# Attention and a gated feed-forward block in one launch: moving the DMA transposes to TensorE, and the copies of the sinks' values to SyncE's queue

## The chip, the core and the metric

The kernel runs on one core of one Trainium2 chip. The metric is the device time in microseconds, from a handful of runs of the compiled kernel. Beside them there is one execution that was taken by the hardware profiler; its span, its rows and its waits are what the views below show.

## The reference

Two parts, one after the other, float32 in and out.

```
scores = (q @ k^T) / 8                       # 4 batches, 8 heads, 768 positions, head dim 64
heads 0, 2, 6 : causal mask                  # the "retrieval" heads
other heads   : causal and (key < 4  or  query - key < 64)   # 4 sinks and a window of 64
x = softmax(scores) @ v   ->  3072 rows x 512
out = (silu(x @ w_gate) * (x @ w_val)) @ w_out       # 512 -> 1536 -> 512
```

## The kernel before

**Tiles.** The rows are cut into 24 tiles of 128 queries. Two neighbouring tiles of a batch make a pair; there are 12 pairs, of which pairs 0 to 5 belong to batches 0 and 1 and pairs 6 to 11 to batches 2 and 3. Four tiles make a group, and the feed-forward part runs by group: six groups of 512 rows.

**Attention of a pair.** SyncE loads 512 KB each of q, k and v (`load`, L341) into one of 11 buffers `raw`. An engine casts q and k to float16 into `hq` (`cast`, L429), and v into `vt` (`castv`, L446). q and k must then be turned, so that the head dimension lies on the partitions (`qT`, `kT`). This is done in two ways:

- pairs 0 to 4 (`XPE = 5`, L336): eight TensorE transposes of 128x128 into one PSUM bank (`transposes`, L469), and two copies out of it by ScalarE or VectorE (`evac`, L475);
- pairs 5 to 11: two transposing DMAs on SyncE's queue (`dmat`, L462), for q as for k. They leave the queries in another order, and `exps` (L569) puts that right by the way it reads and writes (L576).

TensorE then makes the scores (`scores`, L551, its matmuls at L567), ScalarE the exponentials (L579), VectorE or GpSimd multiplies by a mask (L587), TensorE multiplies by the values (`values`, L591, L597), and VectorE divides by the sum into `xb` (`norm`, L600).

**Sinks.** A streaming head sees four sink keys at the start of its batch, and a window. Once a middle tile of a batch has been used, four of its key rows are spent. The keys and values of the sinks are copied into them, so that later tiles find sinks and window in one block of 128 keys. `sinks_v` (L502) does it for the values: two copies of 2 partitions x 330 float16, by VectorE, GpSimd or ScalarE, as the plan says. There are 16 such tiles, hence 32 copies. The `values` of the next tile of the batch wait for them.

**The turned x.** `xb` must be turned too (`xtranspose`, L609). For tiles 0 to 7 (`XBAR = 8`, L423) four TensorE transposes and one copy out of PSUM do it (`xevac`, L624); for tiles 8 to 23 one transposing DMA on SyncE's queue.

**Feed-forward of a group.** For each of 12 slices of 128 columns TensorE makes gate and value products (`gate`, L755, matmuls at L759), ScalarE the tanh (L765), and VectorE two combining steps (L769, L775). The output product is done for groups 0 to 4 with seven half-size products in place of eight (`seventh`, L830, L839; sums of operands at L826, sums of results at L855), for the last group plainly (`outproj`, L788, L793).

**The order.** Everything is a task in a list (`P.add`). The strings `ORDER`, `WAYS` and `SLOTS` were worked out beforehand: `ORDER` gives the tasks in sequence as numbers of two digits to the base 62, `WAYS` the engine of each, `SLOTS` its buffer. Each engine, and SyncE's queue of DMAs, works through its own tasks strictly in that sequence. A number from 3700 up is no task but some filler matmuls on TensorE (`warm`, L315). So a task that waits holds up all that stands behind it on its engine.

Of the kernel before, what the change touches and what calls it, by code (L numbers as in the profile page):

```python
# [13 lines left out]


ORDER = (
    "0306071W091U1V1X000A08xy1c0D0C01050B1d1e040gy01f1gzJ1i1h2021282922232B1j1r1s021p1q1w0F2C2D2E2F1b"
    "2A2L2M2N2O2X2f2g0m1Y1a1Z1t1u1v1k0h252h1l1m2W2c242G2H2I2d2e2l2m2i2j0G271n1o1y1z3C262P2Q2R0z2t3031"
    "2J0y8e8o2n2K102U2o2p3I3J2V8t8j8m8u8v8k8l8n1x2k8f8g8p8q2x382y8h8i118r8s8w8x138y8z9893909495999A33"
    "340n9D9E0E2Z3K3D3L3M3N149B9C9F969G9H972a9192322b2Y2q2r2s2u3R3S3W3X0k1C9c9d9e9h9i9j3U3V3O2z353P36"  # L20
    "39370q1D9f9g9k9l3T3b3i3n3o3f3g0H3H3E3F2v2w0i169I9J9K9N9O9P0o179L9Q9R9M0l1F3Q3Y3Z3c3j3a0I3u40410j"
    "193k3h9m9n9o3l3m3A3B9S9T9U9r9s9t3d3e9X0J3v4344453G3p3q3r0r1G9u9p9v429Y9Z3s3t0x1H2S4647494A4H0p1A"
    "9V9WB74N4O4Q4R0K3z9q9zA10N4c3x4BB4B5B6B8Ak4K4L4V4b4C4D3yAT484M0w0sAQARASAU9a9b9y0t1E0W6K2TAlAmAV"
    "AWAX151M1O1N1PAYAZBEAfAgAhB9BABB4a0u181Q1R1SBCBDAp0v1BBFBGA0AaAbAnAoAc3wBHBIAdAe0L0M0PB20T12A41I"
    "1J1K0S4d4P0O4Z4h4g4Y4e4f5D5L5K0RAzB0B1AqArB31L0YALAM0ZAN4E4F4G4J4I6J1TAuAvAOAPAw9wA2A69xA3A7A55C"
    "5I5JAA4l4m4i4j4kACA8A9ABAD4n4v51524y53AiAj5f5lAEBMAGAFAK4S4z504T4W4UAxAy5g5nAsAtBL4q4r4o4p54BO0c"
    "AHAIAJ4s554t4u4x4wBJBKBQ56575T5U6MBNBP5W5c5XBb5j0X58595A5B707S7T6xBVBW6wBRBS5i5VBXBYBc6z5YBZBaBd"
    "5p5qBT5s605t5u4XBsBtBuCeCbCcCdCfCMCNCOCCBvBwCDCE0V6I5v0Q5F5G5H6v5k5o5M5N5O0UBiBjBk5rCPCQBlBm5E5Z"
    "5a5b5d5wCHCICJCWCXCY5m63696A666768Bh5h73CKCLC7C8C9710eCRCS5P5Q5R6465CACBCTBUC2C36y7Q6P74BnBo5x5y"
    "5z610a72CZCaBp5S625e6H6NBqBrC46B6C6F6D6GCFCGCiBeBfBgBxByBz7O7UC0C1C5C681CUCVCjCl6E6U6V6W6X6Y6R6S"  # L30
    "6T6eDmDjDkDlDnDoDpDqDrDs0b7P7X7WDtDuDv6Z6aCgChCn6b6c6d6fDUDVDWDXDY7576776g7C7D7E7F7G7L0dDwDxCkCm"
    "DSDFDGDHDPDQDRDT7b7c7d6QDADBDCDyDzE0DDDE7H80D5D6D7CsCt6O6n6o6h6i6j6kE1E27V7I7J7M7K7ND8D96l6m7879"
    "7A7BCoCpCrCuCv897Y7Z6p6q8786DKDLDMDZDaDb6L6r6s6t6uDcDdDeDfDgCwCx7e7f7R7j7m7n7o7p7q7rDNDOCyCzD0D4"
    "EhEiEjErEsEcEd88EkElEtCqD1D2D3EuEvEeDhDi7a7g7h7k7iFLFMFNFOFP7x8D8E8A8I8B8C8F8JFJFGFHFIFKFBFCFDDI"
    "DJE5E77s7t8GFEFFEp7u7v7y7w8HEXEYEZ0f838485EmEnEoEqEfEg8NEw8Y8ZE6E88T8U8VEzExEyF0EBE3E9E4EAECEDF6"
    "828K8L8M8OF1F2F3F9EFEG8Q8R8S8W8XEVEHEIEJF7F8FA7l8P7z8a8b8cEaEbESETEUEWEEEOELEM8dGiGMGTGUEKGCENER"
    "G7GVGWGjGkGJGKEPGREQFTFVGXGLGOGPGEGFGNGQG9F4GAGSGGGYGbGZF5GaGcGBGDFSGHFpFqFrFQFRG4G5GdGeFzFUFeFW"
    "FXGIG6G0G8FcFdGfFfFuFvFYFaFbGgGhG1G2G3FsFtFxGlGmFZFwFyFlFiFjFmFnFgFhFkFoGnGoGpGsGtGuGvGwGqGrGxGy"
    "GzH0H2H3H4H5H7H1H6H8H9"
)  # L40
WAYS = (
    "000010000000000000000000000000000000000000000000000000000000221202202202212200200111000111110010"
    "222200001100000000000000220022122022001011000000000000001100212002000011001001000001000001001000"
    "000201021120001000001001000000010010000010000000002221220000000000010000002000100100000020000221"
    "000000000100000002000010010000000000020200000010000000000000110000011000000100100000020001000000"
    "002202200220000000000000000012000100100000000201120000000000000000010002202202010000001001000001"
    "200000000000011002021000000000000000000200000000000000000000000000000000000000000000000000000000"
    "000000000000000000000000000000000000000000001000000000000000000000000000000000000000000000000000"
    "000000000000000000000000000000001000000010000000000000000000000000000000000000000000000000000000"
    "000000000000000000001110100011000000000001000000000000000000000000000000000000000000000000000000"  # L50
    "000000001111000001100000000000100000000000000000000000000000000000000000000000000000000000000111"
    "101100110000000000011000000000000000000000000000000000000000000000000000000000000000010000100000"
    "00000010"
)
SLOTS = (
    "0014237653916A152371476981504A39A2564807049A28352A9168410016041002241601230163620442561014104122"
    "636011642065221025144416322211256461406003404624344620616540610143626540604164236062324342142254"
    "041614064616325426212246140636104325614261306242452460436460636014122636230644521206164434062601"
    "020211341120003102001134000210400214105510131201001011040122021303213020111113411111040020200051"
    "014110101310002114301212131010022102320210013012111032112010000012000102211130011112010111054125"  # L60
    "001050101010110200030111402521014010311140310020120011321112001301101022015010340000101100015042"
    "1331142120102320202014112511225023512531113120100101201"
)
DIGITS = "0123456789ABCDEFGHIJKLMNOPQRSTUVWXYZabcdefghijklmnopqrstuvwxyz"

# [54 lines left out]
def kernel(  # L120
# [13 lines left out]
    nc = tc.nc  # L134
# [198 lines left out]

    XPE = 5  # L336
    XOLD = 1

    landed = {}
# [80 lines left out]
                                 (lambda i=i, x=x: wsum(i, x)),  # L420
                                 deps=[T_w["o", i][0], T_w["o", i + 3][0]] + before))

    XBAR = 8  # L423

    LEAD = 4

    hqs = {}
# [29 lines left out]
    def turned(n, kd):  # L457

        b, pi = QP[n]
        return qT[n % QB] if kd == "q" else kT[b % 2][:, 2 * pi:2 * pi + 2]  # L460

    def dmat(n, kd, m):  # L462
        nc.sync.dma_start_transpose(
            out=turned(n, kd)[:, m].rearrange("c k r (j n) -> c (k r j) n", j=2),
            in_=hqs[n, kd][m * 64:(m + 1) * 64].rearrange("p k a x -> p (k a x)"))

    trs = {}

# [33 lines left out]
    def sinks_v(b, m):  # L502
        V = vt[b % 2]
        for j in range(2):
            rows = slice(j * 64, j * 64 + NSINK // 2)
            recast(T_sv[b, m], V[rows, m, STREAMS], V[rows, 0, STREAMS])

    def plan(t):

# [59 lines left out]
    def exps(t, u, unit):  # L569
        e = es[t, u] = buf("e", [128, 8, 128], FH, "e")  # L570
        for p, s_, c, kt in unit[0]:
            h = PAIRS[p][s_]
            av_blocks.setdefault((t, h), []).append((e[:, c, :], value(t, h, kt)))
        at = slice(min(c for _, _, c, _ in unit[0]), unit[1])
        to, src = e[:, at], whole_sc.pop((t, u))[:, at]
        if t // 2 >= XPE:  # L576
            to = to.rearrange("p c (n j) -> p c n j", j=2)
            src = src.rearrange("p c (j n) -> p c n j", j=2)
        nc.scalar.activation(out=to, in_=src, func=AF.Exp, scale=scale)  # L579

    def mask(task, t, u, m):
# [27 lines left out]
    def xtranspose(t):  # L609
        xb = xbs.pop(t)  # L610
        g, n = GROUP[t]
        if g not in xts:
            xts[g] = buf("xt", [128, 4, 512], FH, "xt")
        if t >= XBAR:
            nc.sync.dma_start_transpose(
                out=xts[g][:, :, n * 128:(n + 1) * 128],
                in_=xb.rearrange("p a b d -> p (a b d)"))
            return
        tr = buf("gv", [128, 4, 128], FH, "xtr")
        for p in range(4):  # L620
            nc.tensor.transpose(tr[:, p, :], xb[:, p].rearrange("p a d -> p (a d)"), ident)
        trs[t] = tr
# [11 lines left out]
    def tasks_of_pair(n):  # L634
# [20 lines left out]
                P.uses(T_iss["x", n], "raw", c)  # L655
        for kd in "qk":
            old = oldq if kd == "q" else older
            if n >= XPE:
                T_ev[n, kd] = [P.lands(P.add(
                    f"d{kd}{n}.{m}", ["SP"], (lambda n=n, kd=kd, m=m: dmat(n, kd, m)),  # L660
                    deps=cs[kd] + old)) for m in range(2)]
                P.uses(cs[kd][0], "hq", *T_ev[n, kd])
                continue
            tr = P.add(f"tr{kd}{n}", ["PE"], (lambda n=n, kd=kd: transposes(n, kd)),
                       deps=cs[kd], takes=["gv"], after=[T_warm])
            T_ev[n, kd] = []
# [8 lines left out]
    def tasks_of_tile(t):  # L675
# [50 lines left out]
        if 1 <= i < NT - 1:  # L726
            T_sk[b, i] = P.add(f"sk{b}.{i}", ["DVE", "POOL", "ACT"],
                               (lambda b=b, i=i: sinks_k(b, i)), deps=own)
            T_sv[b, i] = P.add(f"sv{b}.{i}", ["DVE", "POOL", "ACT"],
                               (lambda b=b, i=i: sinks_v(b, i)), deps=T_v_of[b, i])  # L730
        g, n = GROUP[t]
        lead = T_first_x.get(g)
        takes = [] if lead else ["xt"]
        if t < XBAR:
            xt = P.add(f"xtr{t}", ["PE"], (lambda t=t: xtranspose(t)),
                       deps=norms, takes=["gv"] + takes, after=[lead])
            T_xe[t] = P.add(f"xe{t}", ["DVE", "ACT"], (lambda t=t: xevac(t)), deps=[xt])
# [282 lines left out]
```

## Time and profile before

| | |
|---|---|
| median of 3 runs | 246.04 us (245.84 to 246.38) |
| the profiled execution | 246.15 us, of which the span is 244.4 us |
| granted TensorE clock in it | 1.00 over the whole span |
| VectorE, ScalarE, GpSimd busy | 186.7, 148.5, 129.0 us |
| DMA transposes | 14 of kT, 14 of qT, 16 of xt |
| TensorE transposes | 80 at L473 (q, k), 32 at L621 (x) |
| copies of the sinks' values (2x330 float16) | 18 by ScalarE, 8 by VectorE, 6 by GpSimd |

The rows give a line of the kernel, an engine, and what is written and read. "Busy" of TensorE is not the same as working at full rate: its matmuls are pipelined, their ends are modelled, and short stalls lie inside busy time. Therefore the prediction counts matmuls, and uses the time of long unbroken stretches for each kind. A time in the chain of waits is the time until the next link begins.

### The profile page before, as it was taken

The page shows a single profiled execution, that of the slowest core. Times are in us where ns is not written, and L with a number is a line of the kernel's source. Part 1 is how long each engine was busy: PE and PEld are TensorE (multiplying, and loading weights), DVE is VectorE, ACT ScalarE, POOL GpSimd, SP SyncE. Part 2 cuts the span into 40 slices and gives each one's busy share as a digit, 9 for nine tenths or more (in the row PEclk, how much of TensorE's full clock was granted, in tenths as well). Part 3 has the DMA queues.
Part 4 walks back from the last instruction along what each step waited for, and adds up shares of the span by engine and source line. Part 5 has one row for each costly group of instructions (what it writes and reads, how often), then busy time and mean ns, then how long its engine had stood idle before and what let it go on. Part 6 is the DMA issues. An engine that isn't in the chain of part 4 may idle for free.

```text
span 244.4 us, 5604 instructions
## 1 busy us (share of the span) xinstructions
PE 234.5 (96%) x2189; PEld 143.6 (59%) x2189; DVE 186.7 (76%) x324; ACT 148.5 (61%) x235; POOL 129.0 (53%) x140
## 2 busy tenths in 40 slices
PE   7989999998999999799999999999999999999995
PEld 3667855553457678445555457656456764475743
DVE  0577887889999999887987977669769777776800
ACT  3899899887878669487637776563682302330011
POOL 7479999956497552375765446910094110375000
PEclk9999999999999999999999999999999999999999
DMA  6999999999766989999464451519100213100053
GB/s 187 355 348 353 323 352 366 313 362 305 206 131 78 287 165 289 191 268 192 89 130 130 97 120 38 90 36 234 38 4 0 46 21 115 59 0 1 7 203 136
DMA packets 66794, 40.73 MB, mean 167 GB/s; under 512 B 25168, under 2 KB 60240, under 8 KB 66768
## 3 DMA queue, kind: packets, MB, share of 16 engines
q1 hardware_dynamic: 65392, 37.76, 61.5%
q10 hardware_dynamic: 1376, 2.62, 2.9%
q8 instruction: 17, 0.28, 0.5%
q14 instruction: 9, 0.07, 0.1%
HBM read 28.31 MB, written 6.29 MB: 142 GB/s over the span
## 4 chain that ended last, share of the span: by engine, by line
PE 54%; DVE 19%; issue 8%; DMA 6%; POOL 5%; SPq 5%; ACT 2%; DVEq 0%; POOLq 0%
PE banks L759 34%; PE banks L839 10%; PE banks L793 4%; DMA raw<-in_moe_w_val_dram 4%; DVE h_sb L775 4%; PE banks L567 3%; DVE h_sb L826 3%; SPq L349 3%; DVE sil L769 3%; PE banks L597 2%; POOL hs_sb L826 2%; DVE out_sb L855 2%; DVE xb L605 2%; DMA xt<-xb 2%; DVE e L587 2%
## 5 line engine op out<-in xcount | busy, mean ns | idle before, releaser
L759 PE MATMUL banks<-xt,wg_sb 128*128 128x512 f16 (+1 forms) x304 | 70.3, 368 | 1.9 <-DMA xt<-xb 1.4
L759 PE MATMUL banks<-xt,wv_sb 128*128 128x512 f16 (+1 forms) x304 | 70.4, 368 | 0.8 <-DVE sil L769 0.7
L579 ACT ACTIVATE e<-banks 128x1024 f16<-128x1024 f32 (+2 forms) x68 | 58.7, 910 | 20.0 <-PE banks L567 11.7
L765 ACT ACTIVATE sig<-banks 128x512 f32<-128x512 f32 (+1 forms) x76 | 43.0, 577 | 43.5 <-PE banks L759 37.5
L769 DVE SCALAR_TENSOR_TENSOR sil<-sig,banks 128x512 f32<-128x512 f32 (+1 forms) x76 | 49.0, 656 | 14.8 <-ACT sig L765 12.6
L775 DVE SCALAR_TENSOR_TENSOR h_sb<-sil,banks 128x512 f16<-128x512 f32 (+1 forms) x76 | 48.7, 656 | 6.7 <-PE banks L759 4.4
L587 POOL TENSOR_TENSOR e<-e,m 128x640 f16<-128x640 f16 (+1 forms) x22 | 37.8, 1727 | 27.2 <-ACT e L579 24.3
L759 PEld LDWEIGHTS <-wg_sb 128*128 128x128 f16 x304 | 28.5, 98 | 30.7 <-issue 3.1
L759 PEld LDWEIGHTS <-wv_sb 128*128 128x128 f16 x304 | 28.2, 98 | 29.5 <-issue 1.2
L839 PEld LDWEIGHTS <-h_sb 128*128 128x128 f16 x360 | 34.8, 98 | 7.9 <-issue 0.7
L826 POOL TENSOR_TENSOR hs_sb<-h_sb 128x768 f16<-128x768 f16 x7 | 11.5, 1640 | 40.9 <-DVE h_sb L775 29.4
L855 DVE TENSOR_TENSOR out_sb<-banks,out_sb 128x512 f32<-128x512 f32 x35 | 23.6, 685 | 4.7 <-PE banks L839 4.4
L826 POOL TENSOR_TENSOR h_sb<-h_sb 128x768 f16<-128x768 f16 x11 | 18.0, 1639 | 8.2 <-PE banks L839 4.4
L839 PE MATMUL banks<-wo_sb,h_sb 128*128 128x256 f16 x180 | 21.9, 273 | 0.0
L839 PE MATMUL banks<-wt_sb,h_sb 128*128 128x256 f16 x180 | 21.5, 273 | 0.4 <-DVE out_sb L855 0.4
L567 PE MATMUL banks<-qT,kT 64*128 64x128 f16 x472 | 20.6, 218 | 1.1 <-DVE xb L605 1.0
L567 PEld LDWEIGHTS <-kT 64*128 64x128 f16 x472 | 14.6, 94 | 11.0 <-issue 10.2
L597 PEld LDWEIGHTS <-e 128*128 128x128 f16 x472 | 17.1, 97 | 4.3 <-ACT vt L206 0.9
L597 PE MATMUL banks<-vt,e 128*128 128x65 f16 x472 | 18.2, 193 | 1.0 <-POOL vt L208 0.7
L605 DVE TENSOR_TENSOR xb<-banks,rc 128x512 f16<-128x512 f32 x24 | 16.6, 691 | 0.8
L208 POOL CAST vt<-raw 64x512 f16<-64x512 f32 x22 | 14.4, 654 | 4.8 <-DMA raw<-in_v_dram 2.3
L206 ACT COPY out_sb<-banks 128x512 f32<-128x512 f32 (+1 forms) x7 | 4.0, 570 | 19.1 <-PE banks L793 16.0
(60 smaller groups left out, 216.3 us busy)
## 6 DMA issues: line engine op xcount, KB each, us to landing
raw<-in_v_dram SPq DMA_DIRECT2D x12, 512.0 KB, 7.0
raw<-in_q_dram SPq DMA_DIRECT2D x8, 512.0 KB, 4.8
raw<-in_k_dram SPq DMA_DIRECT2D x8, 512.0 KB, 5.1
raw<-in_moe_w_gate_dram SPq DMA_DIRECT2D x6, 512.0 KB, 8.9
raw<-in_moe_w_val_dram SPq DMA_DIRECT2D x6, 512.0 KB, 8.4
raw<-in_moe_w_out_dram SPq DMA_DIRECT2D x6, 512.0 KB, 7.9
out_dram<-out_sb SPq DMA_DIRECT2D x6, 512.0 KB, 4.7
raw<-in_q_dram SPq DMA_DIRECT2D x8, 256.0 KB, 6.4
```

The source lines that it names most:

```text
L567: nc.tensor.matmul(sc[:, c:c + n, :], weights, moving, start=first, stop=last)
L579: nc.scalar.activation(out=to, in_=src, func=AF.Exp, scale=scale)
L587: ENG[task().way].tensor_tensor(out=ev, in0=ev, in1=mm, op=ALU.mult)
L597: nc.tensor.matmul(avs[t][:, odd, n * 66:n * 66 + 65], ee, vv, start=(m == 0), stop=(m == len(bl) - 1))
L605: nc.vector.tensor_tensor(out=xb.rearrange("p n o d -> p o n d"), in0=av[:, :, :, 0:64], in1=rc.to_broadcast([128, 2, 4, 64]), op=ALU.mult)
L759: nc.tensor.matmul(ps, wsb[:, kk, j * 128:(j + 1) * 128], xt[:, kk, c[0]:c[1]], start=(kk == 0), stop=(kk == 3))
L765: nc.scalar.activation(out=sg[g, j, c], in_=gs[g, j, c], func=AF.Tanh, scale=0.5)
L769: nc.vector.scalar_tensor_tensor(out=sl[g, j, c], in0=sg.pop((g, j, c)), scalar=1.0, op0=ALU.add, in1=gs.pop((g, j, c)), op1=ALU.mult)
L775: nc.vector.scalar_tensor_tensor(out=hs[g, j][:, c[0]:c[1]], in0=sl.pop((g, j, c)), scalar=0.5, op0=ALU.mult, in1=vs.pop((g, j, c)), op1=A ...
L826: ENG[T_hs[g, x][part].way].tensor_tensor(out=to, in0=a, in1=b, op=op)
L839: nc.tensor.matmul(rooms[g, p][:, x], left[:, j, 128 * x:128 * x + 128], right[:, j], start=(j == 0), stop=(j == NK - 1))
L855: nc.vector.tensor_tensor(out=cell(*to), in0=rooms[g, p], in1=cell(*other), op=ALU.add)
```

## The change

Pairs 5 to 11 and tiles 8 to 23 are turned by TensorE as well. `sinks_v` issues two DMAs from SBUF to SBUF on SyncE's queue. The loads of q and k for pairs 5 to 11 take the form that pairs 1 to 4 have: two DMAs of 256 KB with runs of 2 KB, in place of one of 512 KB with runs of 512 bytes. `exps` no longer reorders.

`ORDER`, `WAYS` and `SLOTS` are new. Decoded with the list of tasks, they say: 1099 tasks in place of 1067; the fillers are 25 matmuls in place of 21 (10 + 1, 6, 4, 2, 2 in place of 10 + 2, 4, 5). The number of tasks by engine, where it differs most:

| task | before | after |
|---|---|---|
| copies of turned q and k (`evac`) | ScalarE 12, VectorE 8, DMAs 28 | ScalarE 33, VectorE 15 |
| copies of turned x (`xevac`) | ScalarE 2, VectorE 6, DMAs 16 | ScalarE 13, VectorE 11 |
| sinks' values (2 instructions each) | ScalarE 9, VectorE 4, GpSimd 3 | SyncE's queue 16 |
| masks (L587) | VectorE 16, GpSimd 22 | VectorE 11, GpSimd 27 |
| sums of operands (L826) | VectorE 19, GpSimd 21 | VectorE 23, GpSimd 17 |
| casts of q and k | ScalarE 12, VectorE 3, GpSimd 13 | ScalarE 6, VectorE 5, GpSimd 17 |
| casts of v | ScalarE 16, VectorE 10, GpSimd 22 | ScalarE 19, VectorE 8, GpSimd 21 |

On SyncE's queue the first four sink tasks stand among the first loads: `x2, sv0.1, g0, k3, g1, v1, q3, g4, v4, g2, sv0.2, v2, x3, g5, q4, sv0.3, g3, k4, v5, sv0.4` (x is the attention's v, g and v the two weights).

```diff
-    XPE = 5
+    XPE = 12
...
-    XBAR = 8
-
...
-    def dmat(n, kd, m):
-        nc.sync.dma_start_transpose(
-            out=turned(n, kd)[:, m].rearrange("c k r (j n) -> c (k r j) n", j=2),
-            in_=hqs[n, kd][m * 64:(m + 1) * 64].rearrange("p k a x -> p (k a x)"))
...
-            recast(T_sv[b, m], V[rows, m, STREAMS], V[rows, 0, STREAMS])
+            nc.sync.dma_start(out=V[rows, m, STREAMS], in_=V[rows, 0, STREAMS])
...
-        if t // 2 >= XPE:
-            to = to.rearrange("p c (n j) -> p c n j", j=2)
-            src = src.rearrange("p c (j n) -> p c n j", j=2)
...
-        if t >= XBAR:
-            nc.sync.dma_start_transpose(
-                out=xts[g][:, :, n * 128:(n + 1) * 128],
-                in_=xb.rearrange("p a b d -> p (a b d)"))
-            return
...
-            if n >= XPE:
-                T_ev[n, kd] = [P.lands(P.add(
-                    f"d{kd}{n}.{m}", ["SP"], (lambda n=n, kd=kd, m=m: dmat(n, kd, m)),
-                    deps=cs[kd] + old)) for m in range(2)]
-                P.uses(cs[kd][0], "hq", *T_ev[n, kd])
-                continue
...
-            T_sv[b, i] = P.add(f"sv{b}.{i}", ["DVE", "POOL", "ACT"],
-                               (lambda b=b, i=i: sinks_v(b, i)), deps=T_v_of[b, i])
+            T_sv[b, i] = P.lands(P.add(f"sv{b}.{i}", ["SP"],
+                                       (lambda b=b, i=i: sinks_v(b, i)),
+                                       deps=T_v_of[b, i] + T_v[QP.index((b, 0)), 0]))
...
-        if t < XBAR:
-            xt = P.add(f"xtr{t}", ["PE"], (lambda t=t: xtranspose(t)),
-                       deps=norms, takes=["gv"] + takes, after=[lead])
-            T_xe[t] = P.add(f"xe{t}", ["DVE", "ACT"], (lambda t=t: xevac(t)), deps=[xt])
-            P.uses(xt, "gv", T_xe[t])
-            P.uses(norms[0], "xb", xt)
-        else:
-            xt = P.add(f"xdma{t}", ["SP"], (lambda t=t: xtranspose(t)), deps=norms,
-                       takes=takes, after=[lead])
-            T_xe[t] = P.lands(xt)
-            P.uses(norms[0], "xb", T_xe[t])
+        xt = P.add(f"xtr{t}", ["PE"], (lambda t=t: xtranspose(t)),
+                   deps=norms, takes=["gv"] + takes, after=[lead])
+        T_xe[t] = P.add(f"xe{t}", ["DVE", "ACT"], (lambda t=t: xevac(t)), deps=[xt])
+        P.uses(xt, "gv", T_xe[t])
+        P.uses(norms[0], "xb", xt)
...
```

More of the change, by code (lines that the diff above doesn't have):

```diff
@@ L16 @@
 ORDER = (
[L17 to L36, printed above, removed]
@@ L37 @@
-    "G7GVGWGjGkGJGKEPGREQFTFVGXGLGOGPGEGFGNGQG9F4GAGSGGGYGbGZF5GaGcGBGDFSGHFpFqFrFQFRG4G5GdGeFzFUFeFW"
-    "FXGIG6G0G8FcFdGfFfFuFvFYFaFbGgGhG1G2G3FsFtFxGlGmFZFwFyFlFiFjFmFnFgFhFkFoGnGoGpGsGtGuGvGwGqGrGxGy"
-    "GzH0H2H3H4H5H7H1H6H8H9"
+    "06071U1V0004010903xx1c1W1Xy21f1g1h0A1dzI1i1j1e1p1r1w1q202128292A1s22232B2CzG2E2F2D2L2M2N2O2S050C"
+    "2W2c2d2e02081a1b1Z1Y1t1u1v1k1l0D2X2f2g2l2m2i2j2h2txi2x2y300B2726241m1n1y1z1o252G2H2I2P2Q2R0m109B"
+    "119L312J2K2n2o2p33342U2V0E2Z2Y2b2a1x380g0y98999A9C0z9N9I9O9P9J9K9M9D9E9F2k2q2r2s0G3D3L3M3N9G9H0h"
@@ new lines @@
+    "139X9c9d9e9Y9Z9S9T0n149a9b9f9V9g9U9W0F3C3I3J3K0k1CABACADA6A7A8323R3S3U3V0q0i161DAEA9AFAA2z3O3P3W"
+    "2u353X36379h9i9j9m9n9o0o0H3H3E3b3n3f3g3i3o0l1F179p9q9u0I9r9s9t9v3F9k9l3Q3T393Y3j3Z3aAGAHAI3u9Q9R"
+    "3l3m0j199w3G0J3h3kAL9x9yAMAN2v2w3d3A3e3B400r3c3p3q3r3v431GAJAK3s3tAOAPATAV0p1A9zA04142444546494A"
+    "4H47480x1HBW0s12BTBUBVBXBiBjBk0v1B1I1KApAqArBlBmAzB00u180w1EB11JB4B5B60t151O4O4P4C4D1SB2B31MA1A2"
+    "A3BCBEBFB7B8BG0Y0O5I4L4M4N1L4R4S0M4b0SAsAt0L4aBHBI4BB9BABBBDA4A5ASAU4j4k4l0P5JAuAvAw1Q1R1TBJBKBL"
@@ new lines @@
+    "0N4d4c4Q4W2TBYBZBa4g4h0K3w3z3x3y4fBg0dAxAyBbBc4iBdBeBfBh0X7DAQARAWAX1N1PAiBq4e4p4m4z0U4E4n4F4I4q"
+    "4o4r4GAYAZAbAaAcAd4u4vAeAfAj4J4K4T4U4V5354554s4t0W6YAgAhAkAoBOBPBQBRBS5O5P5QBMBNBpBr5R5S5T7E5B56"
+    "Bn5758AlAm5q5y5z604X4w4x4yC3Bo5C5U5V595A5c5dBv0R5p5v5w5152BtBx505D5EBsBuC1By5F5G5f5l5g5hAnBw6V5x"
+    "5H4Y4ZBzC0C2C40Q5N5K5M5LD30T5u5s5tCbCcCd64616C62D0D1D2D40a7kCqCrCs65660c7o7pCMCNCOD5D66M6N0Z7H7G"
+    "67CtCuD75rD8D97J7K7LCgChCi7IC5C6C77M7N7O0VCv5e5i5j5m5k68CWCXCeCfCY6G6HCRCS5W5X5Y5ZCPCQCT6W6e6f6g"
@@ new lines @@
+    "CjCk6X63696A6B6I7mClCmCnCoCp0e6J6K6L7a7bCCCDCE5a5b5n5o6E6FCw0b7lCF6D6O6P6S6QCGCxCHCI6b6cCK6T6U8R"
+    "6dCyCzCJCLDCDE6R6h6p6q6iCUDoDpDq7cCZCa7P7Q7R6k6u6lEDEEEFC8C9CADyDzDrDsE0CBDhCVDDDF6mEGEH7t7u7vE1"
+    "E2EL6n6o7q7r7sDADGDH6jDeDfDBDgDiENEOEPEIEJEKEMDZDaDbDcDd7X6aDtDuDv7gESETEU6r7Y6s6t7ZDMDN7F7z8081"
+    "717273EQER7S7T7U6v7d7e7fDODP7w877x6y6z70E3E4E574757677E8E9DwDxEA0f8UE6E76w7i7V7W7j6xEVEW8Q8W8X8Y"
+    "8ZEBEC7n6Z78797A7y8a8bDIDJDLDK8H8I82838B8C8DDSDT7h848588867BDQDRDUDY7CFBFLFMFNFOFPFCFDFpFqFrFEFF"
@@ new lines @@
+    "8E8F8GFkFlFmF6F7F8DVDWDX8M8f8c8d8e8k8l8g8hFaFb8TFnFsFtFcFVFW8J8K8L8p9192F9FAFXDjDk8S8w8x8y8i8jFo"
+    "DlEnF1F2Dm898ODn8PF38AEZEbF4F5FGFHFIFfFgFdFe8N8m8n8q8oEXEYEfEgEaEcEeEi8t8z90FhFY8u8vFJFK8r8sFQFi"
+    "FjElFRFS8V939495EdEjEhEpFxEkEmEqEoErEv96FTFUEsEt97GsGxGyGvHCH0GtGuGiGjFZH2GzH1H5GTEuHDHEGbGkEzGU"
+    "H3FzGwH4GYGZEwH6GdGaExGcEyGeGgHAGqF0GfFwGhFuG1FvGnGoGpGJGKGMGWGrGLH7H8GOFyG0GNG8GVGPG6GXGQG7G9G2"
+    "G5G3GRGSHFHGGCGDH9HBGlGmGAGBG4GFGGGHGEGIHHHIHJHMHNHKHOHLHPHQHRHSHTHWHUHVHXHYHbHZHaHcHd"
@@ L40 @@
 )
 WAYS = (
[L42 to L51, printed above, removed]
@@ L52 @@
-    "101100110000000000011000000000000000000000000000000000000000000000000000000000000000010000100000"
-    "00000010"
+    "000000000000000000000000000000000000000000000000000000000000222022200222002200010111100001110110"
+    "222201100000000000000000000122222221000011000000100000000000221220011001001001000000001001001000"
+    "000000221201000000001001000000010000010000000000002202020010000010010000000010010010000010000100"
+    "200000000010010000000000100100000000000001120000000100100000001001000200110200200100000100000000"
@@ new lines @@
+    "000100100000000200022210000101000100100000002000001001000000001020000000001001000010000010001001"
+    "221222000000000001000001000000000000001001222100011000000000000000010010000010000000010000000000"
+    "000000000000000000000000000000000000000000000000000000000000000000000000001100001100000000000000"
+    "000000000000000000000000000000000000000000000000000000000000101000100010000000000011000000000000"
+    "000000000000000000000000000000000000000000000000010010010000000000000000000000000000000000000000"
@@ L54 @@
+    "000000000000000000000000000000000000001011010000000000000000000000000000000000000000000000000000"
+    "000000000000000000000000000101111000100000000000001000000000000000000000000000000000000000000000"
+    "00000000000000000001000000000100000000"
 )
 SLOTS = (
-    "0014237653916A152371476981504A39A2564807049A28352A9168410016041002241601230163620442561014104122"
-    "636011642065221025144416322211256461406003404624344620616540610143626540604164236062324342142254"
-    "041614064616325426212246140636104325614261306242452460436460636014122636230644521206164434062601"
@@ L59 @@
[L59 to L62, printed above, removed]
+    "0015237469308915316843124928706715A09A1604A8273525976A401016041004122601230163424442521540016221"
+    "246001206365222211464624140614432420656023430624140212064634562021114260236140544256162613030440"
@@ new lines @@
+    "411123644040242416263625644045612300063206522203024426341600413164224636161224224560416131226364"
+    "624011045614420604606345426114000310020215114300021041025012510004101112110043001212000015014004"
+    "001131213115000321132020211320214105110001032014201100521240122412131012100001430110124102210203"
+    "025210020213011211400141010010502251225024011010241113312020100005031423400211115010200030013311"
+    "2501531000023112120111122135143040214124512340223024101130201024511300230022210110201"
```

## The prediction

> **What bounds the kernel now.** I read the page first: the span and the busy times.
>
> ```profile
> span 244.4 us, 5604 instructions
> PE 234.5 (96%) x2189; PEld 143.6 (59%) x2189; DVE 186.7 (76%) x324; ACT 148.5 (61%) x235; POOL 129.0 (53%) x140
> ```
>
> TensorE (PE) is busy 96% of the time, but stalls hide inside that. So I went to the chain of waits and took from it, for each kind of matmul, the time of one unbroken stretch (columns: start, length, what, how many instructions).
>
> ```profile
> 28.34 0.45 PE banks L473 x8
> 45.64 0.22 PE banks L621 x4
> 49.97 0.55 PE banks L567 x16
> 96.40 4.70 DMA xt<-xb
> 195.05 0.84 PE banks L597 x28
> 197.62 2.62 PE banks L839 x24
> 200.24 13.81 PE banks L759 x64
> 230.99 10.40 PE banks L793 x60
> ```
>
> One matmul of 512 columns takes 13.81/64 = 0.216 us on the path, one of L839 0.109, a transpose 0.056, scores 0.034, values 0.030. With the counts of the groups by line: L759 544 x 0.216 = 117.4 and 64 of half width x 0.108 = 6.9; L839 420 x 0.109 = 45.9; L567 472 x 0.034 = 16.2, with 2.3 for its mask matmuls; L597 472 x 0.030 = 14.2; L793 10.4; L473 80 x 0.056 = 4.5; L621 32 x 0.055 = 1.8; the fillers, ten cold ones in 4.3 and eleven at 0.216, 6.7. Sum: 226.3 us of TensorE work. As a test, the windows from 140 to 180 us hold 120 matmuls of L759, 72 of L839, 94 of L567 and 93 of L597; at these prices they make 39.8 of 40 us, and nothing stalls there. So the prices are good.
>
> The timeline has the first matmul at 1.36 us and the last copy starting at 241.47, so head and tail are 1.4 + 2.9 = 4.3 us. 244.4 - 4.3 - 226.3 = 13.8 us are stalls. The first gate matmul starts at 20.53 with 16.6 us of work done: 20.5 - 1.4 - 16.6 = 2.5 us stalled before it. The other 11.3 us lie in two stretches, cut where group 2's gates begin:
>
> ```profile
> 20.53:101.24 80.71, 77.80 (x820) 51.14 (x818) 73.62 (x133) 66.43 (x103) 56.02 (x54) 1.00 1.00 263
> 101.24:244.40 143.16, 138.75 (x1148) 81.10 (x1148) 102.89 (x171) 66.06 (x107) 59.22 (x49) 1.00 0.41 93
> ```
>
> (Length; busy PE, PEld, DVE, ACT, POOL; clock, DMA share, GB/s.) In the first, the plan holds 73.7 us of TensorE work in 80.7: 7.0 stalled, with VectorE busy 73.6. In the second, 135.9 us of work in 143.2 - 2.9: 4.4 stalled. The kernel is bound by TensorE, with a stretch at 40 to 100 us where VectorE presses as well. The DMA engines are full until about 65 us and far from it after.
>
> **The change, part by part.** *Transposes, TensorE.* Added: 7 pairs x 2 x 8 = 112 at L473, and 16 tiles x 4 = 64 at L621: 176 x 0.056 = 9.8 us. They are on the bounding engine; only an existing stall can hide them. The Trainium skill (VectorE: DVE Perf Modes, The three transpose paths) gives 390 ns for a 128x128 transpose on TensorE and 1309 for one by DMA, so by it TensorE is the cheaper place. By 390 ns the sum would be 68.6 us; the rows show 56 in a stream, and they decide. But the preference misleads here: the DMA's time was spent on engines with room, and TensorE's comes out of the bound.
>
> *Fillers.* 25 in place of 21: 4 x 0.216 = 0.9 us, partly in waits of the first 20 us; I take 0.4, ends 0 and 0.9.
>
> *Copies out of PSUM, against copies of sinks.* The rows are:
>
> ```profile
> L206 ACT COPY qT<-banks 128x512 f16<-128x512 f16 x8 | 4.5, 590 | 0.1
> L208 DVE COPY xt<-banks 128x512 f16<-128x512 f16 x6 | 2.4, 419 | 0.1
> L206 ACT COPY vt<-vt 2x330 f16<-2x330 f16 x18 | 8.3, 460 | 5.1 <-PE banks L597 4.9
> ```
>
> Added: for q and k 21 x 0.59 on ScalarE and 7 x 0.64 on VectorE; for x 11 x 0.59 and 5 x 0.42: 25.5 us. Removed: 32 copies, 8.3 + 3.8 + 3.2 = 15.3 us. The added copies go mostly to ScalarE, which is busy in 66.1 of the 143 us after 101; that is the cover, and without it each would cost its 0.59. The new plan also hands five masks to GpSimd and takes four sums back. Summed by the rows' durations up to group 2's first gate, VectorE has 87.5 us of work in place of 92.1, TensorE 93.0 in place of 90.3. The cost beside TensorE's is nothing, ends 0 and +3 (30 more PSUM banks are taken, each for a transpose and one or two copies; the waits show only 1.1 us of gates waiting for a bank).
>
> *DMA transposes removed.* 44 issues of about 1.2 us leave SyncE's queue; the casts no longer wait for landings. On TensorE's path one landing shows: 4.70 us for the last tile of group 2, of which TensorE idled 1.4. The replacement is 0.22 + 0.42. Next late there is VectorE's work, which ended at 95.85. The 14 loads split in two add 14 x 0.6 us of issue on a queue that gave up 53 us: nothing.
>
> *Exponentials.* No reordering for later pairs: 22.65 us for 26 before 60 us and 23.93 for 28 after 110. 0.87 and 0.85 a piece, in a mix of sizes: nothing, ends -0.5 and 0 (28 x 0.02).
>
> *Sinks by DMA.* 32 issues of 0.6 us on SyncE's queue, each task waiting for a tile's values on TensorE; behind sv0.1 is queued g0, behind sv0.2 v2, behind sv0.3 g3, behind sv0.4 v3. The next tile's values wait on TensorE, in order, so a late landing stops everything. The nearest row is the landing of what shares the queue:
>
> ```profile
> raw<-in_moe_w_gate_dram SPq DMA_DIRECT2D x6, 512.0 KB, 8.9
> raw<-in_moe_w_val_dram SPq DMA_DIRECT2D x5, 512.0 KB, 8.3
> ```
>
> These are the medians between 10 and 35 us. A small transfer alone is nearer to the 64 KB store's 1.6 us. The Trainium skill (DMA: Bandwidth & Descriptors, Queues, rings and completion order) says each DMA engine takes descriptors in ring order; so a small transfer stands behind the loads issued before it. This rule speaks against the change. The new order puts this much TensorE work between the values that release a sink task and those that need it: sv0.2 8.5 us, sv0.3 5.4, sv0.4 4.7; sv0.1's source is done long before. With 1.2 of issue and 8 of landing, 9.2, they fall short by 0.7 + 3.8 + 4.5 = 9 us; with 1.6 of landing, by none. Later ones have 4.5 us or more, against some 1.2 + 3: none. I take 3, as some of those 9 us fall into stalls that exist already; ends 0 and 9.
>
> *Stalls recovered.* A new plan with more freely placed TensorE work can fill gaps. Of the 7.0 us in the first stretch I give back half, 3.5, for VectorE's relief and the lost 4.7 us landing; of the 4.4 later, 3. Together 6.5; ends 0 and 11.3.
>
> The sum against the profiled execution: 244.4 + 9.8 + 0.4 + 3.0 - 6.5 = 251.1 span. It stood at 246.15, 1.75 over its span, and 0.1 over the median: 251.1 + 1.75 - 0.1 = 252.75, so 252.8 us.
>
> **The rivals.** *Sinks late.* Two or three landings stop TensorE for 3 to 5 us each, as the loads' rows would have it: 9 in place of 3, so 258.8 us. For it: order and landing times. Against: the plan may know the queue, and only 2 partitions are moved. Chance 0.2.
>
> *The gaps swallow it (the other side).* The mechanism: TensorE's stalls after the first gate, 11.3 us, come from VectorE's congestion and DMA landings, both relieved, and transposes slide into them. Work is 237.0 us after; 237.0 + 4.3 + 2.5 before the first gate = 243.8 at best, 245.4 us measured. It decides from the point where fewer than 0.6 us of stalls remain after the first gate, or where the start gets shorter by as much. For it: the 4.70 us landing and VectorE's 4.6 us less. Against: the loads still arrive at the same rate, and no long order here runs free of stalls before 100 us. Chance 0.1, of which 0.07 beats 246.04 by over 0.2%, and 0.03 is within.
>
> *Copies become the bound.* If the 44 copies hold back scores and gates (each in the chain for 0.59 us where a DMA ran unseen), a sixth of 25.5 us, 4.3, comes on top: about 257. Against: ScalarE is half idle after 100 us. Chance 0.08.
>
> **How the numbers follow.** The likeliest case, with 0.62, is TensorE's work on the path with part of the stalls filled: from all 11.3 recovered (4.8 less, 248) to half of the 6.5 (3.2 more, 256). The range holds that, most of the late sinks, and a little below: 247 to 259. Faster 0.07, same 0.03, slower 0.90; 0.2%, 0.5 us, is about what a measurement of this kernel can tell from no change.
>
> **What would show it.** Right: 192 and 96 transposes at L473 and L621 in stretches of 0.056 each; the work summed as above near 237; a span longer by less than 10 us; the page's idle time before L759 no longer released by xt's DMA. Sinks: TensorE idle before L597, released by a DMA vt<-vt, between 30 and 50 us; none if I charge too much. Wrong: a start before the first gate that is shorter than 20.5 us by more than 2, or stretches after 101 us whose stalls vanish while VectorE has gaps; and, on the other side, waits of gates for copies by ScalarE.

## The result, and the profile after

The changed kernel takes 267.69 us (266.07 to 268.11) where the kernel before takes 246.06 on the same chip: a ratio of 1.087, with an interval of 1.082 to 1.091. I had predicted 252.8 us, with a range of 247 to 259. The direction was right; the size was not, 21.6 us in place of 6.8, and the time lies outside the range. One of the runs below, the profiled one of the sinks alone, was over 1.5% slower than the fastest of its kernel and is left out of the times.

The page of the kernel after, in the same rows as that of before, with TensorE's row in 40 slices and the granted clock under it (6.65 us a slice):

```profile
span 266.0 us, 5959 instructions
PE 248.5 (93%) x2369; PEld 154.3 (58%) x2369; DVE 200.6 (75%) x341; ACT 151.9 (57%) x236; POOL 129.7 (49%) x134
PE   7988899999998999909999999999999999999894
PEclk9999999999999999986999999999999999999998
L466 PE MATMUL banks<-ident,hq 128*128 128x128 f16 x192 | 14.8, 223 | 6.8 <-DVE sil L743 6.8
L587 PE MATMUL banks<-vt,e 128*128 128x65 f16 x472 | 17.7, 193 | 0.0
```

There is one slice in which TensorE does almost nothing (the 0 in the middle), and the clock falls in and after it. The idle time before L466, the transposes of q and k, is 6.8 us, and it was VectorE that ended it. The last row answers the question about the sinks: the values never waited for a landing.

The timeline of the kernel after around that slice, VectorE's rows, then GpSimd's, then TensorE's (start, length, what; in brackets the idle time before it):

```profile
110.76 8.22 DVE L577 TENSOR_TENSOR e<-e,m 128x640 f16<-128x640 f16 x1
118.90 0.67 DVE L743 SCALAR_TENSOR_TENSOR sil<-sig,banks 128x512 f32<-128x512 f32 x1
```

```profile
109.57 1.28 POOL L208 CAST vt<-raw 64x512 f16<-64x512 f32 x2
110.82 4.19 POOL L577 TENSOR_TENSOR e<-e,m 128x1024 f16<-128x1024 f16 x2
114.96 1.04 POOL L208 CAST hq<-raw 128x1024 f16<-128x1024 f32 x1
115.94 0.62 POOL L208 CAST vt<-raw 64x512 f16<-64x512 f32 x1
116.51 2.12 POOL L577 TENSOR_TENSOR e<-e,m 128x1024 f16<-128x1024 f16 x1
```

```profile
119.63 1.01 PE L466 MATMUL banks<-ident,hq 128*128 128x128 f16 x8 [6.83 <-DVE sil L743]
```

A mask multiplication on VectorE lasts 8.22 us. The shortest of its shape takes 0.48, and the longest mask on VectorE in the kernel before 1.36 us. Throughout, GpSimd works without a gap: a cast, two masks, a cast, a cast, a mask, until 118.63; VectorE's mask ends 0.3 us later. Behind it VectorE's queue holds the combining step `sil`, which frees the PSUM bank that TensorE's next transpose wants. TensorE, in order, stands 6.83 us.

What the pause costs beyond itself is in the chain of waits of the kernel after:

```profile
119.63 1.01 PE banks L466 x8
120.64 1.71 PE banks L733 x4
122.35 2.47 PE banks L813 x12
124.82 0.45 PE banks L466 x8
125.26 0.86 PE banks L733 x4
```

The same eight transposes take 1.01 us right after the pause and 0.45 five microseconds later; four matmuls of L733 take 1.71 and then 0.86. Until 124.8 TensorE runs at about half its rate (the granted clock is 0.50 from 117.8 to 124.5): 5.19 us for work that takes 0.45 + 0.86 + 12 x 0.109 = 2.6. So the hole costs 6.8 + 2.6 = 9.4 us on TensorE alone.

### The profile page after: what moved, and what is told of

The parts are those of the page before. It is cut to its first block, busy times and chain, and to the rows that moved or that the text cites. A ratio compares the mean times of both kernels' runs of the same rounds, so it can differ in the third digit from the quotient of the medians.

```text
span 266.0 us, 5959 instructions
## 1 busy us (share of the span) xinstructions
PE 248.5 (93%) x2369; PEld 154.3 (58%) x2369; DVE 200.6 (75%) x341; ACT 151.9 (57%) x236; POOL 129.7 (49%) x134
## 4 chain that ended last, share of the span: by engine, by line
PE 67%; DVE 11%; DMA 9%; issue 6%; ACT 3%; POOL 2%; SPq 2%; DVEq 0%; POOLq 0%; ACTq 0%
PE banks L733 33%; PE banks L813 14%; PE banks L560 6%; PE banks L767 4%; PE banks L587 4%; DMA raw<-in_moe_w_gate_dram 3%; PE banks L466 3%; DMA raw<-in_v_dram 3%; DVE sil L743 3%; PE banks L321 3%; ACT e L569 2%; DMA raw<-in_k_dram 2%; PE banks L606 1%; DVE h_sb L749 1%; DMA raw<-in_q_dram 1%
## 5 line engine op out<-in xcount | busy, mean ns | idle before, releaser
L733 PE MATMUL banks<-xt,wg_sb 128*128 128x512 f16 (+1 forms) x304 | 71.2, 371 | 1.1 <-POOL wg_sb L208 0.8
L733 PE MATMUL banks<-xt,wv_sb 128*128 128x512 f16 (+1 forms) x304 | 71.4, 368 | 0.4 <-DVE out_sb L208 0.4
L569 ACT ACTIVATE e<-banks 128x1024 f16<-128x1024 f32 (+2 forms) x68 | 58.9, 912 | 21.6 <-PE banks L560 20.1
L577 POOL TENSOR_TENSOR e<-e,m 128x1024 f16<-128x1024 f16 (+1 forms) x27 | 48.4, 1802 | 27.1 <-ACT e L569 26.9
L733 PEld LDWEIGHTS <-wg_sb 128*128 128x128 f16 x304 | 28.5, 98 | 29.4 <-issue 1.5
L733 PEld LDWEIGHTS <-wv_sb 128*128 128x128 f16 x304 | 28.1, 98 | 28.4 <-issue 0.7
L813 PEld LDWEIGHTS <-h_sb 128*128 128x128 f16 x360 | 34.2, 98 | 7.1 <-issue 1.1
L800 POOL TENSOR_TENSOR h_sb<-h_sb 128x768 f16<-128x768 f16 x10 | 16.4, 1644 | 37.8 <-DVE hs_sb L800 31.1
L560 PE MATMUL banks<-qT,kT 64*128 64x128 f16 x472 | 21.7, 218 | 1.4 <-DVE xb L595 0.5
L466 PE MATMUL banks<-ident,hq 128*128 128x128 f16 x192 | 14.8, 223 | 6.8 <-DVE sil L743 6.8
L208 POOL CAST hq<-raw 128x1024 f16<-128x1024 f32 (+1 forms) x17 | 15.8, 939 | 5.3 <-DMA raw<-in_k_dram 3.0
L466 PEld LDWEIGHTS <-hq 128*128 128x128 f16 x192 | 12.2, 100 | 10.5 <-issue 7.1
L587 PEld LDWEIGHTS <-e 128*128 128x128 f16 x472 | 16.7, 97 | 2.4
L587 PE MATMUL banks<-vt,e 128*128 128x65 f16 x472 | 17.7, 193 | 0.0
L577 DVE TENSOR_TENSOR e<-e,m 128x640 f16<-128x640 f16 (+1 forms) x11 | 15.4, 1401 | 2.4 <-ACT e L569 2.4
```

Source lines behind the costliest of these rows:

```text
L466: nc.tensor.transpose(tr[:, j], hqs[n, kd][:, j // 4, j % 4], ident)
L560: nc.tensor.matmul(sc[:, c:c + n, :], weights, moving, start=first, stop=last)
L577: ENG[task().way].tensor_tensor(out=ev, in0=ev, in1=mm, op=ALU.mult)
L587: nc.tensor.matmul(avs[t][:, odd, n * 66:n * 66 + 65], ee, vv, start=(m == 0), stop=(m == len(bl) - 1))
L733: nc.tensor.matmul(ps, wsb[:, kk, j * 128:(j + 1) * 128], xt[:, kk, c[0]:c[1]], start=(kk == 0), stop=(kk == 3))
L800: ENG[T_hs[g, x][part].way].tensor_tensor(out=to, in0=a, in1=b, op=op)
```

## The experiments

The expectations were written before each run. Times are medians of four runs where nothing else is said, ratios are against runs of the kernel before on the same chip in the same series (medians 246.08 to 246.47).

**The mask to GpSimd.** One digit of `WAYS`; nothing else differs from the changed kernel.

```diff
-  WAYS of mask14.1: VectorE
+  WAYS of mask14.1: GpSimd
```

> The changed kernel with one mask (tile 14, unit 1) on GpSimd in place of VectorE, nothing else. Theory A (VectorE's mask of two SBUF operands was shut out by five GpSimd instructions in a row, 8.2 us for 0.5, and TensorE then ran cold): the hole at 112 to 119 us goes, 7 us of idle and some 2.5 us of slow clock with it: 267.7 - 9.5 = 258.2, within 256.5 to 260. Theory B (the hole is a late exponential or load that the mask waits for, or SyncE's queue): it stays or moves, 265 to 268.

Measured: 257.46 us (256.84 to 258.35), ratio 1.045 (1.043 to 1.047), so 10.2 us less than the changed kernel. Its page:

```profile
span 255.6 us, 5960 instructions
PE 245.9 (96%) x2369; PEld 153.5 (60%) x2369; DVE 192.4 (75%) x340; ACT 152.0 (59%) x236; POOL 130.9 (51%) x135
PEclk9999999999999999999999999999999999999999
```

VectorE is busy 8.2 us less, the length of that one mask, and the granted clock has no dip. The hole is this one instruction's doing. 257.5 lies inside the range that I gave, in part by errors that cancel (see below).

**A shorter train on GpSimd.** On the changed kernel, the two casts in the middle of GpSimd's train go to ScalarE; VectorE keeps the mask.

```diff
-  WAYS of ck8, cx8.0.0: GpSimd
+  WAYS of ck8, cx8.0.0: ScalarE
```

> The changed kernel with the mask of tile 14 still on VectorE, and two casts of the GpSimd train beside it (ck8 and cx8.0.0) on ScalarE, so that three masks of 2.1 us stand in a row there. Theory A (VectorE waits until GpSimd has a gap, not until one instruction ends): the mask lasts about 6.5 us in place of 8.2, and the time falls by some 2 us to 265 to 267. If it gets its turn after one GpSimd instruction: about 2.6 us, and the time near 260. If the mask's length has nothing to do with GpSimd: 8.2 us still.

Measured: 267.68 us (one run), where I had expected 265 to 267. VectorE's mask, then GpSimd's rows:

```profile
111.19 7.01 DVE L577 TENSOR_TENSOR e<-e,m 128x640 f16<-128x640 f16 x1
118.13 0.67 DVE L743 SCALAR_TENSOR_TENSOR sil<-sig,banks 128x512 f32<-128x512 f32 x1
```

```profile
109.69 1.93 POOL L208 CAST vt<-raw 64x512 f16<-64x512 f32 x3
111.60 6.26 POOL L577 TENSOR_TENSOR e<-e,m 128x1024 f16<-128x1024 f16 x3
```

GpSimd's train now ends at 117.86, and the mask ends with it again, 0.3 us later. It was held from the rest of a cast through three whole masks, and not only until the one instruction ended that was under way. The one run shows no gain: the hole closed only 0.8 us earlier, and ScalarE has the two casts in addition.

A pause of GpSimd is not always needed, though. In the changed kernel itself a sum of two SBUF operands on VectorE got its turn between two GpSimd instructions that follow each other without a gap (VectorE, then GpSimd):

```profile
61.62 0.71 DVE L412 TENSOR_TENSOR wt_sb<-wo_sb 128x512 f16<-128x512 f16 x1 [0.24 <-ACT wo_sb L206]
```

```profile
60.89 1.15 POOL L412 TENSOR_TENSOR wt_sb<-wo_sb,wt_sb 128x512 f16<-128x512 f16 x1
62.00 2.45 POOL L412 TENSOR_TENSOR wt_sb<-wo_sb 128x512 f16<-128x512 f16 x2
```

GpSimd's first sum ends at 62.04 and VectorE's 0.3 us later. The mask of 1.36 us in the kernel before, of shape 128x1024, got through in the same way. In all the traces kept, only masks of shape 128x640 were passed over at such a change, and every VectorE instruction with two SBUF inputs got its turn where GpSimd left a gap of 0.04 us or more. What decides who goes first without a gap stays open.

**The added transposes, issued twice.** On the kernel with the mask moved, each of the 176 added transposes is issued a second time into the same place (the output stays what it is).

```diff
-        for j in range(8):
+        for j in list(range(8)) * (2 if n >= 5 else 1):
...
-        for p in range(4):
+        for p in list(range(4)) * (2 if t >= 8 else 1):
```

> The changed kernel with the mask of tile 14 on GpSimd (257.5 us), and each of the 176 added TensorE transposes (pairs 5 to 11, tiles 8 to 23) issued twice. Theory A (TensorE is the bound, its work comes out in full): 176 x 0.056 = 9.8 us more, 267.3 (265.5 to 269). Rival (stalls take up most of it): 258 to 262.

Measured: 266.75 us (266.15 to 267.16), 9.3 more than with the mask moved: 0.053 us for each (0.055 by the two ratios), all of it on the path. No gap took up any of it. This prices a second set beside the first; that the first set costs as much is inferred from it.

**The sinks back on engines.** On the kernel with the mask moved, `sinks_v` copies by ScalarE, VectorE and GpSimd as before (9, 4 and 3 tasks); first placed about 1 us of TensorE work behind the values that release them, then about 60% of the way to the values that need them.

```diff
-            nc.sync.dma_start(out=V[rows, m, STREAMS], in_=V[rows, 0, STREAMS])
+            recast(T_sv[b, m], V[rows, m, STREAMS], V[rows, 0, STREAMS])
```

> The changed kernel with its mask of tile 14 on GpSimd (257.5 us), and the sinks' values copied by the engines that did it before (9 tasks on ScalarE, 4 on VectorE, 3 on GpSimd), placed about 1 us of TensorE work behind the tile that frees the rows. Theory A (in this plan the sinks' DMAs are hidden): no gain from taking them back, 257 to 260, as 15 us of copies return to the engines. Theory C (their landings or the queue behind them cost some of the 11 us that are left): 250 to 255.

> As e6 (the changed kernel, mask of tile 14 on GpSimd, sinks' values copied by engines), but each copy about 60% of the way, in TensorE's work, from its source to its reader. Theory A (the sinks' DMAs cost nothing in this plan, the copies fit in too): 257 to 260. Theory C (the DMAs cost some of the 11 us that are left): 250 to 255.

Measured: 265.7 us (264.27 to 266.21) and 261.46 (261.37 to 261.57). The early placing was a bad one, as the timeline of the first kernel shows:

```profile
23.45 0.96 POOL L208 COPY vt<-vt 2x330 f16<-2x330 f16 x2 [4.03 <-PE banks L587]
```

GpSimd stood 4.03 us for the values, with the cast of a weight queued behind, and the gate matmuls that need it began at 27.97 in place of 24.49. Placed halfway, the copies cost 4.0 us against the DMAs. Both times lie above the 257 to 260 that I had expected if the copies fit in. So the DMAs save about 4 us in this plan, in a comparison with one hand-made placing.

**Each part alone in the old plan.** To the kernel before I did one part at a time, once in the place that the old order gives (where the DMA stood), and for the transposes once later (about 2.6 us of TensorE work behind the norm for x, about 2.2 us behind the casts for q and k). One of the three edits each:

```diff
-            recast(T_sv[b, m], V[rows, m, STREAMS], V[rows, 0, STREAMS])
+            nc.sync.dma_start(out=V[rows, m, STREAMS], in_=V[rows, 0, STREAMS])
...
-    XBAR = 8
+    XBAR = 24
...
-    XPE = 5
+    XPE = 12
```

> The kernel before with its own plan; only the sinks' values go by DMA on SyncE's queue. Theory A (sinks are harmless): within 1 us of 246, or a little less, since 15 us of copies leave ScalarE, VectorE and GpSimd. Theory C (landings behind the loads stop TensorE, as my prediction priced at 3, up to 9): 249 to 255, with TensorE idle before the values matmuls at 30 to 50 us.

> The kernel before with its own plan; only tiles 8 to 23 of x are turned by TensorE and copied out by ScalarE, in the places where their DMAs were issued. Theory A (TensorE is the bound, its work adds up): 64 transposes x 0.055 = 3.5 us, less the 1.4 us of the awaited landing: 248 (247 to 250). A rival (gaps take them up, and the landings were the cost): 244 to 246.

> The kernel before with its own plan; only q and k of pairs 5 to 11 are turned by TensorE and copied out by ScalarE, in the places where their DMAs were issued; their loads are split as in the change. Theory A: 112 x 0.056 = 6.2 us, so 252 (250 to 254). A rival (ScalarE's 28 copies of 0.59 hold up the exponentials and tanh): above 256. The other rival (gaps take them up): 246 to 248.

> The kernel before with its own plan; tiles 8 to 23 of x turned by TensorE, but each group of four transposes placed about 2.6 us of TensorE work behind its norm (where the buffers allow), and its copy 0.5 us further. Theory A (e4's 27 us were TensorE standing, in order, behind VectorE's norms, not the transposes' price): 248 to 253. If it stays above 262, the transposes of x cost far more than their 3.5 us in this plan for another reason.

> The kernel before with its own plan; q and k of pairs 5 to 11 turned by TensorE, each pair's transposes about 2.2 us of TensorE work behind the place of its DMAs. Theory A (e5's 27 us were TensorE standing, in order, behind casts): 6 us of transposes and a few of waits, 252 to 258. Above 265, they cost more in this plan than their place explains.

| part alone | median us (range) | ratio (interval) |
|---|---|---|
| sinks by DMA (three runs) | 286.76 (284.46 to 288.37) | 1.163 (1.156 to 1.170) |
| x in place | 273.35 (271.75 to 274.05) | 1.110 (1.107 to 1.113) |
| x later | 255.59 (255.42 to 257.15) | 1.041 (1.037 to 1.045) |
| q and k in place | 273.14 (272.13 to 273.36) | 1.108 (1.105 to 1.110) |
| q and k later | 260.68 (260.08 to 260.83) | 1.059 (1.057 to 1.061) |

All five lie above the range of my theory A, and the sinks above that of theory C too. With the transposes TensorE's work grows by 64 x 0.055 = 3.5 and 112 x 0.056 = 6.2 us; the rest is waits and, with the transposes in place, a mean granted clock of 0.98 to 0.99. With x in place, TensorE's waits (us, times, longest) begin with:

```profile
PE banks L621 <- DVE xb L605: 11.4, 8, 2.8
PE banks L759 <- ACT xt L206: 5.0, 5, 2.0
```

A DMA may be put right behind the norm and waits on its queue; a transpose there makes TensorE wait for the norm, and the gates behind it for the copy. With q and k in place it waits 12.2 us, in seven waits, for their casts. Two or three microseconds of other TensorE work in between took away 17.8 us for x and 12.5 for q and k. What is left in the later places is in good part waits for ScalarE's copies out of PSUM, 4.5 us for x and 7.1 for q and k. So in the old plan the copies do hold TensorE up, as my third rival feared for the new one.

For the sinks alone the price is the highest, 40 us. In its trace SyncE's queue stands 63.7 us, in ten waits, for TensorE's values, with loads queued behind. GpSimd waits up to 8.8 us for a load, and TensorE three times (6.2, 6.0 and 5.6 us) for what GpSimd casts. For the sinks themselves it waits less:

```profile
PE banks L597 <- DMA vt<-vt: 5.5, 3, 2.9
```

The mean granted clock of the three runs is 0.945 to 0.952, so part of the price is slow clock behind the pauses.

**DMA transposes again in the new plan.** The mask moved, the sinks still by DMA, and x, or q and k, or both turned by DMA again, the DMAs right behind norm and casts; in the fourth kernel both, at the places of the transposes that they replace.

```diff
+    XBAR = 8
...
-    XPE = 12
+    XPE = 5
...
+            nc.sync.dma_start_transpose(
+                out=xts[g][:, :, n * 128:(n + 1) * 128],
+                in_=xb.rearrange("p a b d -> p (a b d)"))
```

> The changed kernel with its mask of tile 14 on GpSimd (257.5 us), and x of tiles 8 to 23 turned by DMAs again, each issued right behind its norm (for a group's first tile: when its buffer is free). Theory A (the transposes cost what they occupy on TensorE, 0.053 to 0.055 each): 64 x 0.054 = 3.5 us less, 254 (252.5 to 256). Rival (the DMAs' landings hold up the gates as one did before): 256 to 259.

> The changed kernel with its mask of tile 14 on GpSimd (257.5 us), and q and k of pairs 5 to 11 turned by DMAs again, each issued right behind its cast (and behind the last reader of the rows it writes). Theory A: 112 x 0.054 = 6.0 us less, 251.5 (250 to 254). Rival (sinks waiting on SyncE's queue hold the transposing DMAs behind them, and the scores wait): 255 or more.

> The changed kernel with its mask of tile 14 on GpSimd (257.5 us), and both x and q, k turned by DMAs again; of the change only the sinks' DMAs and the new order are left. Theory A: 176 x 0.053 = 9.3 us less, 248.2 (246.5 to 251). If the sinks' DMAs were worth something by themselves (15 us of copies off the engines), it comes out under 246; if the new order is worse in itself, above 251.

> As e11 (the changed order and sinks by DMA, mask of tile 14 on GpSimd, x and q, k turned by DMAs again), but each DMA stands where the plan has its TensorE transpose, mostly 5 us of TensorE work or more before its first reader. Theory A (e9 to e11 lost their time to SyncE's queue standing behind casts): 9.3 us less than 257.5 and some short landings (five with under 3 us), 248 to 254. If it stays above 265, DMA transposes and sinks on one queue don't go together in this plan, wherever they stand.

Measured: 283.88 us (ratio 1.155, interval 1.151 to 1.159), 319.53 (1.300, 1.296 to 1.303), 334.19 (1.358, 1.355 to 1.360) and 296.57 (1.203, 1.199 to 1.208), all far above the 257.5 us of the kernel that they start from. My theory fell here. TensorE's waits in the fourth:

```profile
PE banks L597 <- DMA vt<-vt: 18.9, 5, 7.4
...
PE banks L760 <- DMA xt<-xb: 5.8, 3, 3.8
```

Five waits for the sinks' DMAs, up to 7.4 us each, that the changed kernel does not have. SyncE's queue goes in order: a sink task waits for TensorE's values, a turning DMA for a cast or a norm, and each holds all that follows. In the orders that I tried the two kinds do not go together; whether a newly made order could fit both was not tried.

**The one landing that was on the path.** In the kernel before, only tile 9, whose landing showed as 4.70 us, is turned by TensorE with a copy by VectorE.

```diff
+    XTE = (9,)
...
-        if t >= XBAR:
+        if t >= XBAR and t not in XTE:
...
-        if t < XBAR:
+        if t < XBAR or t in XTE:
```

> The kernel before with its own plan; only tile 9 of x, whose landing held up group 2's first gate by 1.4 us, is turned by TensorE at the place of its DMA, and copied by VectorE. If that wait was worth its length: 1.4 - 0.6 = 0.8 us less, 245.3. If TensorE's idle there is taken over by the next late thing (VectorE's steps, which ended at 95.9): within 0.4 us of 246.1.

Measured: 248.99 us (248.92 to 249.09), ratio 1.011 (1.009 to 1.013). VectorE's rows, then TensorE's:

```profile
100.34 1.41 DVE L856 TENSOR_TENSOR out_sb<-banks,out_sb 128x512 f32<-128x512 f32 x2
101.66 0.55 DVE L827 TENSOR_TENSOR h_sb<-h_sb 128x768 f16<-128x768 f16 x1
...
102.50 0.42 DVE L208 COPY xt<-banks 128x512 f16<-128x512 f16 x1
```

```profile
102.98 1.86 PE L760 MATMUL banks<-xt,wg_sb 128*128 128x512 f16 x4 [2.42 <-DVE xt L208]
```

The transposes are done soon after 100.5, but the copy stands in VectorE's queue behind sums until 102.50. TensorE's wait there grew from 1.4 to 2.42 us. The landing was late, and what comes next was later. The same matmuls in the kernel before:

```profile
101.24 1.02 PE L759 MATMUL banks<-xt,wg_sb 128*128 128x512 f16 x4 [1.36 <-DMA xt<-xb]
```

They took 1.02 us there, and 1.86 here: the granted clock is 0.50 from 102.98 to 105.80, while it stayed at 1.00 behind the wait of 1.36 us. An estimate from these figures: 1.1 us more of waiting and half of 2.8 us, 1.4, make 2.5 of the 2.6 us that this kernel loses. Both of my expectations, 245.3 and some 246.1, were too low.

## Why the prediction was wrong

*Transposes, 9.8:* right, as far as doubling shows: a second set costs 9.3 us, 0.053 each, in full. My choice of the row's 56 ns over 390 ns decided this term rightly.

*"The cost beside TensorE's is nothing, ends 0 and +3":* this step failed. I treated the masks that the new plan moves between engines as durations to be summed per engine, and saw VectorE relieved. The five masks that I counted are a balance: nine go from VectorE to GpSimd and four the other way, and the mask that was held, mask14.1, is one of the four. But a mask on VectorE is not a fixed 0.48 us: beside a train on GpSimd it took 8.22, and cost 10.2 us in all. Both facts were open to me, that the plan changes which engine does each mask and which GpSimd tasks stand together, but no mask on VectorE in the kernel before took longer than 1.36 us, and the longest sum of two SBUF operands 1.75 (0.55 alone). Its trace warned of such holds, but not of this size. The Trainium skill names the mechanism (SBUF — State Buffer, Who interferes with whom): a VectorE instruction with two inputs in SBUF contends with a GpSimd instruction that reads SBUF, and whichever is issued second is blocked until the first has finished. By that rule alone the mask, issued at 110.76, would have waited for the cast whose row ends at 110.85; here it was held through five more instructions. That this mask was held until GpSimd paused is shown twice, with trains that ended at 118.63 and 117.86; why it was passed over where other instructions were not is open, and that the shared port is the reason is the skill's account and was not tested by itself.

*"Stalls recovered", 6.5:* mis-sized, it is about nothing. Priced as in the prediction, the changed kernel has 6.4 us of stalls from its first gate (22.25) to group 2's gates (104.20), where the kernel before had 7.0. Afterwards it is 4.8 with the mask moved, in place of 4.4. And before the first gate, it is 3.4 in place of 2.5. Together that is 0.7 us more of stalls, not 6.5 less. The loads of the other engines between first gate and group 2 did fall, as the window of the changed kernel shows (length; busy PE, PEld, DVE, ACT, POOL; clock, DMA share, GB/s):

```profile
22.25:104.20 81.95, 79.25 (x859) 53.15 (x856) 67.92 (x123) 64.26 (x100) 61.19 (x51) 1.00 0.73 241
```

VectorE is busy 67.9 us in place of 73.6, and the DMA share is 0.73 in place of 1.00. TensorE's stalls hardly followed, so a lower sum of either load did not by itself shorten them. (That the DMA engines are far from full after 65 us was misread: in the kernel before their share is still 0.88 from 65 to 101 us, and 0.41 only after that.) The one landing that I counted on hid a later wait, as tile 9 alone shows.

*Sinks, 3:* TensorE waited 0.0 us for them; the lower end was right. SyncE does stand in its queue waiting for values, 77 us in ten waits, but no load behind comes so late that TensorE waits long for it: its longest wait for a cast of a load is 0.8 us. The traces give no landing time for these transfers, so whether one stands behind the loads in its ring is not shown; they were only in time. In the old order the same DMAs cost 40 us: the place decides. And the copies that they replace, which I took as free, would cost about 4 us here, in the better of two hand-made placings.

*Fillers, 0.4:* they were not tried alone. 0.9 us more of work stands before the first gate, which fits all four fillers there counting in full.

*The sum:* 21.6 us = 10.2 for the held mask + 9.3 for the transposes + 2.1 left. Of these 2.1, priced from the trace and not tested, 0.9 are the fillers, 0.7 the stalls, and 0.3 a larger time outside the span (257.64 - 255.6 = 2.04 in place of 1.75); 0.2 is within the scatter. Of the 9.4 us seen on TensorE around the hole and the 10.2 that moving the mask gained, 0.8 I have not traced. Without the held mask the prediction would have missed by 4.7 us: the recovery was 7.2 too large, and the 3 us for the sinks, which were not needed, covered part of that by luck. What the new order is worth by itself stays open: the runs that turn by DMA again in it lose too much to waits to tell.

Of the rivals none was right. The sinks were not late, and the gaps swallowed nothing. No wait of TensorE for a copy of turned q, k or x is above 0.3 us with the mask moved, though that kernel's 257.5 us is near the 257 of the third rival.

No version that I ran beats the kernel before: the best with all transposes on TensorE is 4.5% slower, and of that some 4 points are the transposes themselves.

## What to carry to other kernels

When a plan moves elementwise work with two SBUF inputs onto VectorE beside a busy GpSimd, look at what GpSimd does then and not only at the sum of durations: leave a gap in its train (untried here, but gaps of 0.04 us let such instructions through elsewhere), or give it the instruction. Work added to the bounding engine cost its full price here; do not credit it with stalls until a run shows what these stalls wait for, since the wait behind the last one can be longer. Before a transfer is moved to a queue that goes in order, look at what it waits for and at what stands behind it; and give a transpose moved to TensorE a few microseconds of other work ahead of it, which saved 12.5 and 17.8 us here.

## What the runs showed of the hardware that I had not expected

- A VectorE mask of 0.48 us was held 8.22 us beside six GpSimd instructions in a row, and 7.01 us beside a shorter train, each time until 0.3 us after GpSimd's last. Other instructions with two SBUF inputs, as the sum at 61.62, got their turn without a pause of GpSimd.
- 6.8 us of idle TensorE were followed by some 5 us at half rate (granted clock 0.50; eight transposes 1.01 us, then 0.45), and 2.6 us were lost to that. A wait of 2.42 us, with tile 9 alone, was followed by 2.8 us at 0.50; one of 1.36 us by none.
- 32 small DMAs from SBUF to SBUF on SyncE's queue made TensorE wait 0.0 us in one order and cost 40 us in another.
